# Low parts moved to GpSimd, a block's normed rows turned through DRAM, and a denser first weave

## The chip, the core and the metric

The kernel runs on one core of one Trainium2 chip. Its engines are TensorE (PE in the profile), VectorE (DVE), ScalarE (ACT), GpSimd (POOL) and SyncE (SP), whose queue issues nearly all transfers. The metric is the device time of one execution in microseconds, as the median of several runs.

## What is computed

Two layers, each a hedgehog linear attention and a squared-ReLU MLP, both with a layer norm ahead and a residual around them. S = 2048 rows, D = 576, H = 32 heads of 18, F = 4608.

```python
x = A_x
for layer in range(2):
    n = layernorm(x)
    q, k, v = n @ wqkv                      # split in 32 heads
    phi(u) = concat(softmax(u @ w_phi), softmax(-(u @ w_phi)))
    kv = phi(k)^T v;  z = sum of phi(k) over the rows
    x = x + (phi(q) kv / (phi(q) z + 1e-6)) @ wo
    n = layernorm(x)
    h = relu(n @ w1 + b1)
    x = x + (h * h) @ w2 + b2
```

All is fp32. The kernel holds each operand of a product as a high and a low part (the low is the value less its high part) and makes three products of them.

## The kernel before

The 2048 rows are four blocks of 512 (four tiles of 128 rows each), and a layer takes them in an order of its own: 3, 2, 0, 1 in layer 0 and 1, 0, 3, 2 in layer 1. The MLP of one block runs over 36 feature tiles f of 128 columns. For each tile `first` loads w1's columns and w2's rows and splits them: ACT makes the high parts (L1167 for w1, L1168 and L1169 for w2), DVE the low part of w1 (L1171, 128x640) and of 448 columns of w2 (L1174), POOL the low part of w2's other 128 columns (L1175). `hidden` is the first half of a tile on PE (14 matmuls, L1190); ACT then takes relu (L1197), square (L1198) and the square once more in full (L1199), and DVE the low part of that (L1200); the second half is `by_rows` (12 matmuls, L1217) and `features` (3, L1208), one tile behind the first half as the program is written.

The MLP of a layer's first block is woven with the attention of its second and third: `weave` lets the attention's generators go on by so many units of cost after each of the MLP's 36 yields. In this first weave (names m_3 in layer 0, m_1 in layer 1) run in turn the features of the second block (a_2 in layer 0, a_0 in layer 1), the query products and features of the third (a_0, then a_3), and then, for the second block, the output products (`o_product`: eight of 14 matmuls on PE, L999), the residual sum (`o_add` on DVE, L1004), and the layer norm `g_norm`: statistics on DVE (L459, L462), the root on POOL (L463, L464), the normed rows on DVE (L490, and L495 for the last 64 columns, written twice), x + b2 on POOL (L1051), transposes on PE (L512, L526) and the splits of their results on ACT and DVE (L520, L521, L533, L534). The turned rows, named a_2nh and a_2nl, are the operands of the next block's MLP (m_2), which is the second weave. The output products of a tile go through a few places in PSUM, which DVE's sums empty.

The features of the attention take another way to be turned: DVE transposes in blocks of 32x32 (L897), and stores put the blocks in their order in DRAM (L900), from which they are loaded.

A scheduler sets the order of instructions on each engine at build time. Each engine takes its own list strictly in that order; what is not ready holds what stands behind it.

## Time and profile before

| what | us |
|---|---|
| median of three runs | 2440.04 (2438.57 to 2442.45) |
| the profiled execution | 2441.59, span 2439.9 |
| PE busy | 2410.0 |
| DVE busy | 1560.5 |
| ACT busy | 1289.7 |
| POOL busy | 940.6 |
| first weave, layer 0 | 234 to 502 |
| second weave, layer 0 | 502 to 813 |
| first weave, layer 1 | 1441 to 1710 |
| second weave, layer 1 | 1710 to 2022 |

In a timeline a row holds the start, the time, the engine, the line, the operation, what is written from what, the shapes, and in brackets how long the engine stood idle before it and what it waited for last. Matmuls are pipelined, so that the time of one is longer than the distance to the next; distances between starts tell what PE spends. In a table by window the columns are the window, its length, busy time of the engines, the granted clock of PE (1.00 is full), the share of the transfer engines and GB/s.

### The profile page before, as it was taken

To read this page: it belongs to the slowest core of one execution; us is meant where nothing else is said; L and a number is where in the kernel's file an instruction comes from. 1 tells how busy PE (TensorE), PEld (TensorE's weight loads), DVE (VectorE), ACT (ScalarE), POOL (GpSimd) and SP (SyncE) were. 2 spreads that over 40 slices of the span, in tenths; PEclk is the share of its full clock that TensorE was granted. 3 is DMA by queue.
4 is the path that set the end of the run, shared out by engine and by line. 5 is a ranking of instruction groups with operands and counts; after the bars stand their busy time and mean duration, and the time that the engine had idled before them with its cause. 6 is when DMAs were issued, how large, how long until landed. Compare 5 with 4: busy or idle time off the path is not lost. (4 is left out here: it accounts for less than half of the span.)

```text
span 2439.9 us, 41475 instructions
## 1 busy us (share of the span) xinstructions
PE 2410.0 (99%) x14806; PEld 2137.9 (88%) x14806; DVE 1560.5 (64%) x2537; ACT 1289.7 (53%) x2543; POOL 940.6 (39%) x1121
## 2 busy tenths in 40 slices
PE   9999999999999999999999999999999999999999
PEld 8999888888888888888999988888887888888898
DVE  8779847664867655545766787486557675555443
ACT  4344555444456666664443444554455466676643
POOL 4555303212335565542433442032222455565321
PEclk9999999999999999999999999999999999999999
DMA  9124573666654533338753156537667444333364
GB/s 338 64 84 165 163 194 97 151 202 220 155 173 136 157 99 115 109 104 302 257 188 139 59 173 143 168 96 186 191 233 158 141 142 145 118 103 116 110 199 130
DMA packets 370646, 379.40 MB, mean 155 GB/s; under 512 B 142886, under 2 KB 270790, under 8 KB 367878
## 3 DMA queue, kind: packets, MB, share of 16 engines
q1 hardware_dynamic: 369180, 375.37, 51.2%
q8 instruction: 116, 1.90, 0.3%
q10 hardware_dynamic: 1258, 1.37, 0.2%
q14 instruction: 92, 0.75, 0.1%
HBM read 297.22 MB, written 79.41 MB: 154 GB/s over the span
## 5 line engine op out<-in xcount | busy, mean ns | idle before, releaser
L1507 POOL TENSOR_TENSOR m_ps<-m_pr,m_ps 128x128 fp32r<-128x128 f32 x144 | 98.6, 685 | 337.8 <-ACT m_ps L1505 310.7
L1506 DVE TENSOR_TENSOR m_ps<-m_pr,m_ps 128x448 fp32r<-128x448 f32 x144 | 99.8, 693 | 175.9 <-ACT m_ps L1504 175.8
L1549 PE MATMUL m_pacc<-m_ps,m_phb 128*128 128x448 f32 x864 | 185.6, 363 | 0.0
L1549 PEld LDWEIGHTS m_pacc<-m_ps,m_phb 128*128 128x128 f32 x864 | 161.9, 188 | 15.0
L1549 PE MATMUL m_pacacc<-m_ps,m_phc 128*128 128x448 f32 x648 | 147.1, 365 | 0.0
L1504 ACT ACTIVATE m_ps<-m_pr 128x448 fp32r<-128x448 f32 x144 | 82.8, 575 | 115.7 <-issue 64.9
L1549 PEld LDWEIGHTS m_pacacc<-m_ps,m_phc 128*128 128x128 f32 x648 | 119.2, 188 | 7.7
L1190 PE MATMUL m_0ph<-a_0nh,m_0h 128*128 128x512 f32 (+1 forms) x380 | 96.7, 382 | 1.6 <-ACT m_0hr L1197 1.4
L1190 PE MATMUL m_1ph<-t1onh,m_1h 128*128 128x512 f32 (+1 forms) x380 | 96.2, 381 | 2.0 <-ACT m_1hr L1197 1.8
L1217 PE MATMUL m_2acc<-m_2s,m_2hb 128*128 128x448 f32 x432 | 95.2, 367 | 2.9 <-ACT m_2s L1168 2.6
L1190 PE MATMUL m_3ph<-t0onh,m_3h 128*128 128x512 f32 (+1 forms) x380 | 96.1, 381 | 1.8 <-ACT m_3hr L1197 1.6
L1217 PE MATMUL m_0acc<-m_0s,m_0hb 128*128 128x448 f32 x432 | 95.0, 367 | 2.9 <-ACT m_0s L1168 2.6
L1190 PE MATMUL m_2ph<-a_2nh,m_2h 128*128 128x512 f32 (+1 forms) x380 | 96.6, 382 | 0.8 <-ACT m_2hr L1197 0.6
L1217 PE MATMUL m_3acc<-m_3s,m_3hb 128*128 128x448 f32 x432 | 94.2, 364 | 2.0 <-ACT m_3hb L1198 1.4
L1217 PE MATMUL m_1acc<-m_1s,m_1hb 128*128 128x448 f32 x432 | 94.2, 364 | 2.0 <-ACT m_1hb L1198 1.4
L1217 PEld LDWEIGHTS m_2acc<-m_2s,m_2hb 128*128 128x128 f32 x432 | 81.8, 190 | 11.7 <-ACT m_2s L1168 3.0
L1217 PEld LDWEIGHTS m_0acc<-m_0s,m_0hb 128*128 128x128 f32 x432 | 81.5, 190 | 11.7 <-ACT m_0s L1168 3.0
L1217 PEld LDWEIGHTS m_3acc<-m_3s,m_3hb 128*128 128x128 f32 x432 | 80.4, 188 | 10.6 <-ACT m_3hb L1198 2.1
L1217 PEld LDWEIGHTS m_1acc<-m_1s,m_1hb 128*128 128x128 f32 x432 | 80.4, 188 | 10.5 <-ACT m_1hb L1198 2.1
L1175 POOL TENSOR_TENSOR m_3s<-m_3r,m_3s 128x128 fp32r<-128x128 f32 x36 | 22.9, 637 | 161.9 <-ACT m_3s L1169 153.3
L1175 POOL TENSOR_TENSOR m_1s<-m_1r,m_1s 128x128 fp32r<-128x128 f32 x36 | 22.8, 635 | 162.0 <-ACT m_1s L1169 151.8
L1190 PEld LDWEIGHTS m_1ph<-t1onh,m_1h 128*128 128x128 f32 x380 | 68.8, 188 | 17.4 <-ACT m_1hr L1197 3.0
(2464 smaller groups left out, 7237.0 us busy)
## 6 DMA issues: line engine op xcount, KB each, us to landing
m_pr<-in_B_w SPq DMA_DIRECT2D x144, 288.0 KB
m_pr<-in_B_w SPq DMA_DIRECT2D x72, 256.0 KB
hd<-m_pu SPq DMA_DIRECT2D x72, 256.0 KB
m_pg<-hd SPq DMA_DIRECT2D x72, 256.0 KB
m_3r<-in_B_w SPq DMA_DIRECT2D x36, 288.0 KB
m_2r<-in_B_w SPq DMA_DIRECT2D x36, 288.0 KB
m_1r<-in_B_w SPq DMA_DIRECT2D x36, 288.0 KB
m_0r<-in_B_w SPq DMA_DIRECT2D x36, 288.0 KB
```

Of the source, the lines that this page charges most:

```text
L1175: nc.gpsimd.tensor_sub(s2[:, FC + P : FC + 2 * P], r2[:, R:], s2[:, FC : FC + P].bitcast(F32))
L1190: dense["hidden"] = nc.tensor.matmul(ph[:, cols], a, m, start=(k == 0), stop=(k == len(ops) - 1))
L1217: nc.tensor.matmul(acc[t][:, :R], a[:, rows], m, start=(f == 0 and k == 0), stop=(f == NF - 1 and k == 2))
L1504: nc.scalar.activation(s2[:, RO : RO + R], r2[:, :R], AF.Copy)
L1506: nc.vector.tensor_sub(s2[:, RO + R : RO + 2 * R], r2[:, :R], s2[:, RO : RO + R].bitcast(F32))
L1507: nc.gpsimd.tensor_sub(s2[:, FC + P : FC + 2 * P], r2[:, R:], s2[:, FC : FC + P].bitcast(F32))
L1549: nc.tensor.matmul(accs[b][t][:, :R], a[:, rows], m, start=(g == 0 and k == 0), stop=(g == NF - 1 and k == 2))
```

## The change

It has three parts. The low part of w2's 448 columns moves from DVE to POOL (for the first two tiles of a layer's first block it stays on DVE), in `low`. The norm of the first woven block is no longer `g_norm` but the new `g_norm_far`: one DVE operation norms all 576 columns, one more transposes them in blocks of 32x32, 16 stores per block put the pieces in order in DRAM, one load of 1 MB brings back the first 512 columns turned, `load_twice` the last 64 in two copies, and ACT and DVE split what came back. And the weave's rate goes from 3.7 to 4.2 units per yield.

```diff
--- before.py
+++ after.py
@@ -584,6 +584,56 @@
                 apart(NT - 1)
                 yield 1.6
 
+    def blocks_out(home, flat, t):
+        for i in range(NQ):
+            at = t * P + 32 * i
+            nc.sync.dma_start(home[:, at : at + 32].rearrange("(j f) r -> f j r", f=32),
+                              flat[32 * i : 32 * i + 32].rearrange("f (j r) -> f j r", r=32))
+
+    def g_norm_far(x_of, dst, name, then=None):
+        home = dram.tile([D, TB], F32, name=f"{name}xt")
+        xns, raw = {}, {}
+
+        def rows(t):
+            x = x_of(t)
+            mv, rstd = moments(x, t, name)
+            xns[t] = sb.tile([P, D], F32, tag="qk", name=f"{name}n{t}", bufs=5)
+            nc.vector.tensor_scalar(xns[t], x, mv[:, 0:1], rstd, op0=ALU.subtract, op1=ALU.mult)
+            if then:
+                then(t, x)
+
+        def turn(t):
+            nc.vector.transpose(xns[t], xns[t])
+
+        def store(t):
+            blocks_out(home, xns.pop(t), t)
+
+        def land():
+            dst.update(xt_tiles(name))
+            nc.sync.dma_start(dst["l"].bitcast(F32), home[: KC * P].rearrange("(c p) n -> p c n", p=P))
+            raw["t"] = sb.tile([P, TB], F32, tag="ft", name=f"{name}t", bufs=4)
+            load_twice(raw["t"], home, 0, TB)
+
+        def split(c):
+            if c < KC:
+                hi, src, p = dst["h"][:, c], dst["l"][:, c].bitcast(F32), slice(0, P)
+                lo = dst["l"][:, c]
+            else:
+                hi, src, p = dst["h"][:, c], raw["t"], slice(DT, P)
+                lo = dst["h"][DT:, c]
+            nc.scalar.activation(hi, src, AF.Copy)
+            dense["normed"] = nc.vector.tensor_sub(lo, src[p], hi[p].bitcast(F32))
+
+        yield from pipeline(NT, (rows, turn, lambda t: t < NT - 1 and store(t)), (3.0, 0.9, 0.2))
+        yield 3.0
+        store(NT - 1)
+        yield 3.0
+        land()
+        yield 4.0
+        for c in range(NC):
+            split(c)
+            yield 0.8
+
     def spill(b, x):
         nc.sync.dma_start(xth[b], x["h"].rearrange("p c n -> p (c n)").bitcast(F32))
         nc.sync.dma_start(xtl[b], x["l"].rearrange("p c n -> p (c n)").bitcast(F32))
@@ -895,10 +945,7 @@
         def turn(t):
             flat = ph[t].rearrange("p s d -> p (s d)")
             nc.vector.transpose(flat, flat)
-            for i in range(NQ):
-                at = t * P + 32 * i
-                nc.sync.dma_start(home[:, at : at + 32].rearrange("(j f) r -> f j r", f=32),
-                                  flat[32 * i : 32 * i + 32].rearrange("f (j r) -> f j r", r=32))
+            blocks_out(home, ph[t].rearrange("p s d -> p (s d)"), t)
 
         yield from held(pipeline(NT, (start, lambda t: soft_exp(ph[t]), add, factors, lambda t: phi_scale(ph[t], rs[t]),
                                       turn), (2.6, 0.4, 3.0, 2.8, 1.2, 1.6)), ("last", "squared"))
@@ -1171,7 +1218,7 @@
                 dense["lowered"] = (nc.gpsimd if early else nc.vector).tensor_sub(l1, r1, h1.bitcast(F32))
 
             def low():
-                nc.vector.tensor_sub(s2[:, RO + R : RO + 2 * R], r2[:, :R], s2[:, RO : RO + R].bitcast(F32))
+                (nc.vector if early else nc.gpsimd).tensor_sub(s2[:, RO + R : RO + 2 * R], r2[:, :R], s2[:, RO : RO + R].bitcast(F32))
                 nc.gpsimd.tensor_sub(s2[:, FC + P : FC + 2 * P], r2[:, R:], s2[:, FC : FC + P].bitcast(F32))
 
             if early:
@@ -1839,7 +1886,7 @@
         def back_first():
             m, later = f"a{layer}_{order[2]}", []
             mid = (g_queries(layer, order[2], None, later, m), g_features(layer, later, early, m))
-            yield from g_attend(layer, order[1], None, raws, nxt, f"a{layer}_{order[1]}", dense, None, mid)
+            yield from g_attend(layer, order[1], None, raws, nxt, f"a{layer}_{order[1]}", dense, g_norm_far, mid)
 
         def back_second():
             yield from g_attend(layer, order[2], None, None, operands, f"a{layer}_{order[2]}", None,
@@ -1923,7 +1970,7 @@
                 if last:
                     keep.update(x=xk, es=es, v=wpair("v", f"w{m}"))
 
-        weave(g_mlp(layer, order[0], ready, [], f"m{layer}_{order[0]}", dense.pop("rest")), chained(back_first()), 3.7, "rows")
+        weave(g_mlp(layer, order[0], ready, [], f"m{layer}_{order[0]}", dense.pop("rest")), chained(back_first()), 4.2, "rows")
         back = chained(back_second())
 
         def then():
```

The lines shift by 47 from `first` on: w1's low is L1218 then, w2's L1221 and L1222, the first half L1237, the second L1264 and L1255, relu, square and full square L1244 to L1246, the output products L1046 and their sums L1051. The new lines are L601 (normed rows), L606 (transpose on DVE), L590 (stores), L613 (load) and L624 and L625 (splits).

Three places show how the order of instructions changes. The first is DVE in the first weave of layer 0, where the output products of the last tiles are summed and normed (a_2x rows with the residual, a_2ns and a_2nm their statistics, a_2nn the normed rows, m_3h and m_3s the split w1 and w2 of a feature tile, whose number follows). Before:

```order
L1004 TENSOR_TENSOR a_2x_5698<-a_2po_5716,a_2x_5698 128x288 [waits PE_49]
L459 BN_STATS a_2ns_5732<-a_2x_5698 128x6 [waits DVE_49]
L462 BN_AGGR a_2nm_5733<-a_2ns_5732 128x2 [waits DVE_49]
L490 TENSOR_SCALAR a_2nn_5740<-a_2x_5698,a_2nm_5733,a_2nd_5734 128x512 [waits DVE_49,Pool_49]
L1174 TENSOR_TENSOR m_3s_30_5436<-m_3r_30_5430,m_3s_30_5436 128x448 [waits DMAHW4_49,Activation_49]
L495 TENSOR_SCALAR a_2ne<-a_2x_5698,a_2nm_5733,a_2nd_5734 128x128
L1171 TENSOR_TENSOR m_3h_31_5494<-m_3r_31_5488,m_3h_31_5494 128x640 [waits DMAHW6_49,DMAHW7_49,DMAHW5_49,Activation_49]
L1174 TENSOR_TENSOR m_3s_31_5495<-m_3r_31_5489,m_3s_31_5495 128x448 [waits DMAHW0_49,Activation_49]
```

The last of these rows is the low part of w2 for f=31, and behind it the weave runs on for three more feature tiles before the last two tiles of rows come. With the change:

```order
L1051 TENSOR_TENSOR a_2x_5700<-a_2po_5702,a_2x_5700 128x288 [waits PE_49]
L459 BN_STATS a_2ns_5734<-a_2x_5700 128x6 [waits DVE_49]
L1051 TENSOR_TENSOR a_2x_5700<-a_2po_5718,a_2x_5700 128x288 [waits PE_49]
L459 BN_STATS a_2ns_5734<-a_2x_5700 128x6 [waits DVE_49]
L462 BN_AGGR a_2nm_5735<-a_2ns_5734 128x2 [waits DVE_49]
L601 TENSOR_SCALAR a_2nn_5742<-a_2x_5700,a_2nm_5735,a_2nd_5736 128x576 [waits DVE_49,Pool_49]
L606 STREAM_TRANSPOSE a_2nn_5742<-a_2nn_5742 128x576 [waits DVE_49]
L1218 TENSOR_TENSOR m_3h_28_5351<-m_3r_28_5345,m_3h_28_5351 128x640 [waits DMAHW6_49,DMAHW7_49,DMAHW5_49,Activation_49]
L1247 TENSOR_TENSOR m_3hb_5477<-m_3hr_5476,m_3hb_5477 128x512 [waits Activation_49]
L1218 TENSOR_TENSOR m_3h_29_5453<-m_3r_29_5447,m_3h_29_5453 128x640 [waits DMAHW6_49,DMAHW7_49,DMAHW0_49,Activation_49]
```

The four tiles of rows now stand in one run, the fourth of them shown here, and w1's low for f=28 has moved behind the whole run. No w2 low stands among these rows.

The second place is PE, at the tiles 32 and 33 of the same block (m_3ph the first half's sums, m_3acc the second's). Before:

```order
L1190 MATMUL m_3ph_5564<-t0onh,m_3h_32_5556 128x512 [waits Activation_49]
L1190 MATMUL m_3ph_5564<-t0onh,m_3h_32_5556 128x512 x4
L1190 MATMUL m_3ph_5564<-t0onl,m_3h_32_5556 128x512 x4
L1190 MATMUL m_3ph_5564<-t0onh,m_3h_32_5556 128x512 [waits DVE_49]
L1190 MATMUL m_3ph_5564<-t0onh,m_3h_32_5556 128x512 x4
L1190 MATMUL m_3ph_5662<-t0onh,m_3h_33_5654 128x512 [waits Activation_49]
L1190 MATMUL m_3ph_5662<-t0onh,m_3h_33_5654 128x512 x4
L1190 MATMUL m_3ph_5662<-t0onl,m_3h_33_5654 128x512 x4
L1190 MATMUL m_3ph_5662<-t0onh,m_3h_33_5654 128x512 [waits DVE_49]
L1190 MATMUL m_3ph_5662<-t0onh,m_3h_33_5654 128x512 x4
L1217 MATMUL m_3acc_3539<-m_3s_32_5557,m_3hb_5678 128x448 [waits Activation_49]
```

The second half of f=32 has the first half of f=33 ahead of it. With the change:

```order
L1237 MATMUL m_3ph_5760<-t0onh,m_3h_32_5752 128x512 [waits Activation_49]
L1237 MATMUL m_3ph_5760<-t0onh,m_3h_32_5752 128x512 x4
L1237 MATMUL m_3ph_5760<-t0onl,m_3h_32_5752 128x512 x4
L1237 MATMUL m_3ph_5760<-t0onh,m_3h_32_5752 128x512 [waits DVE_49]
L1237 MATMUL m_3ph_5760<-t0onh,m_3h_32_5752 128x512 x4
L1264 MATMUL m_3acc_3539<-m_3s_32_5753,m_3hb_5831 128x448 [waits Activation_49]
L1264 MATMUL m_3acc_3539<-m_3s_32_5753,m_3hb_5831 128x448 [waits Pool_49]
L1264 MATMUL m_3acc_3540<-m_3s_32_5753,m_3hb_5831 128x448 x2
L1264 MATMUL m_3acc_3541<-m_3s_32_5753,m_3hb_5831 128x448 x2
L1264 MATMUL m_3acc_3542<-m_3s_32_5753,m_3hb_5831 128x448 x2
L1264 MATMUL m_3acc_3539<-m_3s_32_5753,m_3hb_5831 128x448 [waits DVE_49]
```

The second half of f=32 now follows its own first half. So it is for f=28, 33 and 34, and the second half of f=31 stands behind the last three matmuls of f=30. Going back to the run of output products, f=27's second half stands inside it, and f=28's first half right behind it. Further up, the query products of the third block have moved two feature tiles earlier; the direct successions of that region were f=13's two halves and f=14 and 15's first halves, and are now the first halves of f=12 and f=13.

The third place is SP's queue at the end of the same weave, with the fourth tile's stores (a_2nxt is the place in DRAM, m_3r the loaded weights):

```order
L1208 DMA m_3r_33_5802<-in_B_w 128x576 [waits DMAHW0_49,Pool_49]
L590 DMA a_2nxt<-a_2nn_5742 32x18x32 [waits DMAHW1_49]
L590 DMA a_2nxt<-a_2nn_5742 32x18x32 [waits DMAHW2_49]
L590 DMA a_2nxt<-a_2nn_5742 32x18x32 [waits DMAHW3_49]
L590 DMA a_2nxt<-a_2nn_5742 32x18x32 [waits DMAHW4_49]
L1206 DMA m_3r_34_5861<-in_B_w 128x4x128 [waits DMAHW5_49,DVE_49]
L244 DMA m_3r_34_5861<-in_B_w 64x128 [waits DMAHW6_49]
L244 DMA m_3r_34_5861<-in_B_w 64x128 [waits DMAHW7_49]
L613 DMA a_2nl<-a_2nxt 128x4x512 [waits DMAHW2_49,DMAHW3_49,DMAHW1_49,DMAHW4_49,DMAHW0_49,PE_49]
L244 DMA a_2nt<-a_2nxt 64x512 x2
L1208 DMA m_3r_34_5862<-in_B_w 128x576 [waits Pool_49]
```

None of the stores and loads of a_2nxt stood there before; the weight loads around them did. The load of the turned rows now stands between the w1 and the w2 loads of f=34. On ACT, the first two splits (L624) have come to stand behind w1's high part of f=34 and ahead of the relu of f=34.

## The prediction

> **What bounds the kernel now.** I read the page's totals first, then a table by stage, then the waits of TensorE (PE) with its timeline.
>
> ```profile
> span 2439.9 us, 41475 instructions
> ...
> PE 2410.0 (99%) x14806; PEld 2137.9 (88%) x14806; DVE 1560.5 (64%) x2537; ACT 1289.7 (53%) x2543; POOL 940.6 (39%) x1121
> ```
>
> PE is busy for all but 30 us, so a change gains only what it takes from PE's instructions or from those 30 us, and loses what it adds to them.
>
> ```profile
> core 0: us, PE busy (x) PEld busy (x) DVE busy (x) ACT busy (x) POOL busy (x), PEclk, DMA share, GB/s
> 234.00:502.00 268.00, 264.27 (x1314) 229.99 (x1313) 185.04 (x274) 139.12 (x255) 71.20 (x74) 1.00 0.60 157
> 1441.00:1710.00 269.00, 265.07 (x1319) 230.50 (x1318) 186.72 (x276) 139.78 (x257) 71.43 (x74) 1.00 0.59 158
> ```
>
> These stretches are the first weaves of the two layers, where the change lies. Each has under 4 us of idle PE, so there is little to win and everything that opens between matmuls is new time. The idle pieces of layer 0 are these:
>
> ```profile
> 320.31 2.68 PE L1217 MATMUL m_3acc<-m_3s,m_3hb 128*128 128x448 f32 x12 [1.44 <-ACT m_3hb L1198]
> ...
> 327.64 1.45 PE L1190 MATMUL m_3ph<-t0onh,m_3h 128*128 128x512 f32 x5 [0.78 <-ACT m_3hr L1197]
> ...
> 455.05 0.40 PE L999 MATMUL a_2po<-a_2o0h,a_2oh 126*128 126x288 f32 x1 [0.18 <-DVE a_2x L1004]
> ...
> 457.99 1.27 PE L1217 MATMUL m_3acc<-m_3s,m_3hb 128*128 128x448 f32 x5 [0.56 <-DVE m_3s L1174]
> ...
> 471.60 1.45 PE L1190 MATMUL m_3ph<-t0onh,m_3h 128*128 128x512 f32 x5 [0.78 <-ACT m_3hr L1197]
> ...
> 503.95 0.86 PE L1190 MATMUL m_2ph<-a_2nh,m_2h 128*128 128x256 f32 x5 [0.19 <-DVE a_2nl L521]
> ```
>
> They give the two prices that carry my sum. Where the second half of feature tile f stands directly behind its own first half (f=13, at 320.31), PE waits 1.44 us for relu and square on ACT. Where the first half of f+1 stands directly behind the first half of f, it waits 0.78 us for the relu.
>
> **The work that PE does meanwhile.**
>
> ```profile
> 446.79 0.29 PE L999 MATMUL a_2po<-a_2o0h,a_2oh 126*128 126x288 f32 x1
> ...
> 454.26 0.60 PE L512 MATMUL a_2np<-ident,a_2nn 128*128 128x128 f32 x4
> ...
> 459.11 1.29 PE L1190 MATMUL m_3ph<-t0onh,m_3h 128*128 128x512 f32 x5
> ...
> 462.28 0.77 PE L1217 MATMUL m_3acc<-m_3s,m_3hb 128*128 128x448 f32 x3
> ...
> 463.89 2.67 PE L1217 MATMUL m_3acc<-m_3s,m_3hb 128*128 128x448 f32 x12
> ...
> 467.07 0.29 PE L999 MATMUL a_2po<-a_2o0h,a_2oh 126*128 126x288 f32 x1
> ```
>
> Starts against starts: a first half takes 462.28 - 459.11 = 3.17 us, a second half 467.07 - 463.89 = 3.18, and four output products (446.79 to 454.26) 7.47, so one is 1.87. The last three matmuls of a second half are some 0.69 of it.
>
> **Part 1: transposes leave PE.**
>
> ```profile
> L512 PE MATMUL a_2np<-ident,a_2nn x16: 270/272/278, 454.3 to 501.5; 128*128 128x128 f32 x16
> ...
> L526 PE MATMUL a_2np<-ident,a_2ne x4: 272/273/273, 491.9 to 501.7; 128*128 128x128 f32 x4
> ```
>
> ```profile
> 491.07 0.60 PE L512 MATMUL a_2np<-ident,a_2nn 128*128 128x128 f32 x4
> 491.42 0.65 PE L1217 MATMUL m_3acc<-m_3s,m_3hb 128*128 128x448 f32 x2
> ```
>
> The matmuls overlap: four take 0.35 us from start to start, not 4 x 0.27. Twenty take 20 x 0.0875 = 1.75 us a layer. That is the whole direct gain of this part, 3.5 us in both layers.
>
> **Part 2: the DRAM trip.** Sixteen stores, one large load and two tail loads join SP's queue.
>
> ```profile
> 450.37 3.13 SPq L900 DMA_DIRECT2D a_0ft<-a_0Q3e  x4
> ```
>
> ```profile
> 1875.18 10.45 DMA a_2w<-a_2ft
> ```
>
> The same kind of store takes 0.78 us to issue, so 19 issues hold SP for up to 15 us, over some 45 us. Tile 3's stores stand behind the w2 load of f=33, which waits for GpSimd's low of f=31. By the walk of part 3 f=28's w1 low ends 24.7 us after the first output product; f=31's loads follow it, f=31's low on GpSimd comes at some 35, and so the last stores at about 41 and the load at 47 (an estimate). I take 8 to 10 us for the load, from the 10.45 us row (504 KB, the nearest): it is there at about 56. ACT's first split stands behind f=33's squares, by the same walk at about 64. So the trip costs nothing, with 8 us of cover; if the cover is gone, ACT's relu of f=34 is queued behind that split and PE waits one for one.
>
> **Part 3: the denser weave and the order it makes.** The output products of four tiles now come in one run, from f=27 instead of f=29, and nothing is left over to separate the last feature tiles. I walk the new order with the durations above; 0 is the first output product. The durations on DVE and POOL come from their timelines and from the groups of this stage.
>
> ```profile
> 449.96 0.42 DVE L1004 TENSOR_TENSOR a_2x<-a_2po,a_2x 128x288 f32<-128x288 f32 x1
> 450.42 0.46 DVE L459 BATCH_NORM_STATS2 a_2ns<-a_2x 128x6 f32<-128x288 f32 x1
> ...
> 451.76 0.21 DVE L462 BATCH_NORM_AGGREGATE a_2nm<-a_2ns 128x2 f32<-128x12 f32 x1
> 452.97 0.55 DVE L490 TENSOR_SCALAR a_2nn<-a_2x,a_2nm,a_2nd 128x512 f32<-128x512 f32 x1 [1.00 <-POOL a_2nd L464]
> ...
> 458.12 0.81 DVE L1171 TENSOR_TENSOR m_3h<-m_3r,m_3h 128x640 fp32r<-128x640 f32 x1
> ```
>
> ```profile
> L1174 DVE TENSOR_TENSOR m_3s<-m_3r,m_3s 128x448 fp32r<-128x448 f32 x36 | 26.9, 751 | 3.1 <-ACT m_3s L1168 3.0
> ...
> L897 DVE STREAM_TRANSPOSE a_0Q3e<-a_0Q3e 128x1152 f32<-128x1152 f32 x1 | 1.4, 1379 | 0.1
> ```
>
> ```profile
> L1175 POOL TENSOR_TENSOR m_3s<-m_3r,m_3s 128x128 fp32r<-128x128 f32 x36 | 22.9, 637 | 161.9 <-ACT m_3s L1169 153.3 <-DMA m_3r<-in_B_w 5.5 <-DVE m_3h L1171 3.1
> ...
> L1171 POOL TENSOR_TENSOR m_3h<-m_3r,m_3h 128x640 fp32r<-128x640 f32 x2 | 3.1, 1567 | 5.4 <-ACT m_3h L1167 5.4
> ```
>
> - The fifth product waits for a place that DVE must empty. Before, this cost 0.18 behind 0.35 us of transposes; without them 0.5.
> - f=27's second half, in the middle of the products, waits for GpSimd's 128x448 low, which stands behind tile 1's two small POOL steps. No row shows that operation; between POOL's 128x128 (0.64) and 128x640 (1.57) I take 1.2. The low ends about 1.3 us after PE wants it (bounds 0 and 2).
> - f=28's first half needs its w1 low from DVE, which now stands behind the norm and transpose of all four tiles. Eight products, f=27 and the waits so far end at 15.0 + 3.2 + 1.8 = 20.0; nine matmuls of f=28 run on to 22.0. DVE needs from 20.0: add 0.45, stats 0.46, aggregate 0.21, 1.0 for POOL's root, some 0.65 for 576 columns, 0.7 for the transpose (half the 128x1152 row), 0.81 for the low: 24.3, with semaphores 24.7. Wait 2.7 (2.3 to 3.1).
> - Then f=28's second half directly behind its first: 1.44. f=30 behind f=29: 0.78. f=31's second half has only three matmuls ahead of it: 1.44 - 0.69 = 0.75. f=32, 33 and 34 each follow directly: 3 x 1.44 = 4.32.
> - The handover to the next block: one relu wait at most, 0.8 (0 to 0.8).
>
> Together 0.5 + 1.3 + 2.7 + 1.44 + 0.78 + 0.75 + 4.32 + 0.8 = 12.6 us a layer. Against that, the pieces of 455.05, 457.99, 471.60 and 503.95 go (0.18 + 0.56 + 0.78 + 0.19 = 1.7), and so does the 1.44 at 320.31, since the query products now stand between f=13's halves; the 0.78 there stays, between f=12 and f=13. Those query products come two feature tiles earlier (2 x 6.35 us), with their loads far ahead in SP's queue: 0. ACT's splits are five of 512 columns instead of six, beside PE work as before: 0.
>
> **Part 4: w2's low on GpSimd.** 140 subtractions leave DVE (36 in a weave are 26.9 us, 0.75 each; f=0 and 1 of the first block stay). DVE is 64% busy, so its relief is worth nothing by itself. GpSimd does the wide and the narrow part one after the other, 1.2 + 0.64 = 1.8 us, and each tile's matmuls start, less the end of its low, nearly always 7 to 20 us later. Two had no such room: f=30 (at 457.99, counted above) and f=17 in the second weave:
>
> ```profile
> 659.47 0.49 PE L1217 MATMUL m_2acc<-m_2s,m_2hb 128*128 128x448 f32 x1 [2.57 <-ACT m_2s L1168]
> 660.26 3.83 PE L1217 MATMUL m_2acc<-m_2s,m_2hb 128*128 128x448 f32 x11 [0.30 <-DVE m_2s L1174]
> ```
>
> There 1.2 for 0.62, starting a little sooner, adds about 0.45 a layer (0 to 1.3).
>
> **The clock after a long gap.** The row above is also the one gap of the size that I forecast for f=28.
>
> ```profile
> 659.50:660.30 0.80, 0.50 (x2) 0.20 (x2) 0.71 (x2) 0.12 (x1) 0.61 (x1) 0.68 0.83 286
> 660.30:664.00 3.70, 3.70 (x12) 3.33 (x13) 0.62 (x1) 0.78 (x2) 0.92 (x2) 0.61 1.37 204
> 664.00:668.00 4.00, 4.00 (x21) 3.54 (x20) 1.45 (x2) 1.52 (x3) 0.43 (x1) 1.00 0.89 280
> ```
>
> The clock column falls to 0.61 behind it and is back at 1.00 from 664. Half speed over 3.4 us costs 1.7 us. If it comes behind f=28's wait in both layers, 3.4 us are added; I give that half a chance and leave it out of the sum. The Trainium skill, page "TensorE: Matmul & The Clock Gate", section "Part 1: The HAM clock gate", says that the clock is set by a free-running window of about 3.4 us and halves after an idle one; by a threshold of a whole idle window a wait of 2.7 us would never do it and the sum would stand. This trace disagrees: 2.57 us were enough here.
>
> **Sum.** 12.6 - 1.7 - 1.44 - 1.75 + 0.45 = 8.2 us a layer, 16.3 in both. The profiled execution took 2441.6 us (span 2439.9), 1.6 above the median of the runs, 2440.0. So 2441.6 + 16.3 = 2458 by it, 2456 by the median; I say 2457. What is late next: DVE's w1 lows of f=29 and 30 follow f=28's and SP's loads of f=31 and 32 wait for them, still ahead of PE by my count.
>
> **Rivals.**
> - The succession costs nothing, so it ends faster. Its mechanism: DVE and ACT are early enough that relu and square overlap PE's last matmuls. For: DVE loses 27 us of lows in this weave. Against: relu cannot start before the half's last matmul, and the one direct succession in the trace paid 1.44. It decides once the new waits stay under 4.4 us a layer (1.7 + 1.44 + 1.75 - 0.45). With none, 2440.0 - 8.9 = 2431; with 2.5 a layer left, 2436.
> - Only ACT's successions hold, and the DVE and POOL waits of the products (0.5 + 1.3 + 2.7) and the handover shrink to nothing: 12.6 - 5.3 = 7.3, so +2.9 a layer, 2446.
> - The trip lands late. Its price is one for one beyond 64 us; SP's queue, in which stores wait behind weight loads that wait for GpSimd, could be 12 us later than I count. Then ACT holds f=34's relu by 4 us a layer, and 2457 + 8 = 2465.
> - GpSimd becomes late for several feature tiles, because DVE and POOL slow each other:
>
> ```profile
> 458.28 1.95 POOL L1051 TENSOR_TENSOR a_2x<-a_2x,b2t 128x576 f32<-128x576 f32 x1 [1.15 <-DVE a_2ne L495]
> 458.85 1.85 DVE L1174 TENSOR_TENSOR m_3s<-m_3r,m_3s 128x448 fp32r<-128x448 f32 x1
> ```
>
> That 1.85 stands beside a 128x576 sum on POOL. With each low at 2 instead of 1.2 the tightest ones (f=17, 27, 28) pay 0.8 each: 2.4 a layer, 2462. The Trainium skill, page "SBUF — State Buffer", section "SBUF: two separate sides", calls the port pair of the two engines an exclusive lock, held for a whole instruction, which these two rows bear out.
>
> **From these to the numbers.** My forecast, with or without the halved clock (2457 to 2460): 0.57. Late trip: 0.12. Late GpSimd: 0.08. Successions alone: 0.10. Faster: 0.13. The range of 8 in 10 leaves out most of the faster case and the far end of the late ones: 2437 to 2466. Within 0.2% (4.9 us), which is about what a measurement can tell from no change, lie a half-faster case and the low edge of the successions: 0.10. Faster 0.13, slower 0.77.
>
> **What would show it.** Right: PE idle of 12 to 13 us in each first weave instead of 3.7, with 1.4 us pieces released by the square before f=32, 33 and 34, and one of some 2.7 us released by DVE in f=28; no matmul into a_2np; ACT's first split of a_2nh without a DMA wait. Wrong: pieces under 0.5 us before those tiles, or a DMA as releaser of ACT, or stalls in the second weave on POOL.

## The result and the profile after

The changed kernel took 2485.13 us (median of four runs, 2482.92 to 2485.49), beside 2440.26 us (2438.57 to 2442.45) for the kernel before on the same chip. The ratio is 1.0181, with a 95% interval from 1.0164 to 1.0199. The forecast was 2457 with a range of 2437 to 2466: the direction came out, the size did not. 17 us were expected, 45 came. I begin with the page of the changed kernel and the table by stage:

```profile
span 2483.1 us, 41200 instructions
...
PE 2423.2 (98%) x14766; PEld 2141.4 (86%) x14766; DVE 1491.7 (60%) x2395; ACT 1290.4 (52%) x2541; POOL 1092.1 (44%) x1261
```

```profile
core 0: us, PE busy (x) PEld busy (x) DVE busy (x) ACT busy (x) POOL busy (x), PEclk, DMA share, GB/s
234.00:502.00 268.00, 254.92 (x1239) 219.28 (x1239) 161.15 (x227) 128.94 (x233) 105.07 (x103) 0.99 0.59 150
1441.00:1710.00 269.00, 259.26 (x1328) 225.48 (x1327) 175.22 (x273) 127.54 (x239) 111.68 (x113) 0.98 0.58 149
...
456.00:462.50 6.50, 5.06 (x14) 4.09 (x13) 2.68 (x3) 3.87 (x7) 2.59 (x3) 0.50 0.88 212
507.00:510.20 3.20, 2.91 (x8) 2.61 (x9) 3.17 (x4) 2.07 (x5) 2.36 (x3) 0.53 0.31 81
...
1685.00:1695.00 10.00, 7.76 (x19) 6.16 (x20) 3.42 (x4) 3.87 (x7) 4.48 (x5) 0.50 0.66 158
```

PE's idle time has grown from 30 us to 60 (span less busy), and PE is also *busy* 13 us longer, with 40 matmuls fewer. The second part is seen in the last three rows: behind two of the gaps of layer 0, and behind the like of the first in layer 1, the granted clock is about 0.5. (The second row covers other work than the row with the same times before, since everything there is some 24 us later.) The waits of PE in the first weave of layer 0, and the costliest of them in the timeline (in square brackets: the idle time ahead of a piece and what ended it):

```profile
engine line waited for: us in total, times, longest us
PE m_3acc L1264 <- ACT m_3hb L1245: 5.1, 4, 1.4
PE m_3ph L1237 <- DVE m_3h L1218: 3.6, 1, 3.6
PE m_3ph L1237 <- ACT m_3hr L1244: 2.7, 3, 1.1
PE m_3acc L1264 <- ACT m_3s L1215: 2.3, 1, 2.3
PE m_3acc L1264 <- POOL m_3s L1221: 1.4, 2, 1.0
```

```profile
247.70 1.43 PE L1237 MATMUL m_3ph<-t0onh,m_3h 128*128 128x512 f32 x5 [1.09 <-ACT m_3hr L1244]
...
440.80 2.08 PE L1264 MATMUL m_3acc<-m_3s,m_3hb 128*128 128x448 f32 x9 [1.03 <-POOL m_3s L1221]
...
454.91 1.59 PE L1237 MATMUL m_3ph<-t0onh,m_3h 128*128 128x512 f32 x5 [3.56 <-DVE m_3h L1218]
457.93 4.85 PE L1264 MATMUL m_3acc<-m_3s,m_3hb 128*128 128x448 f32 x12 [1.44 <-ACT m_3hb L1245]
...
489.23 2.68 PE L1264 MATMUL m_3acc<-m_3s,m_3hb 128*128 128x448 f32 x12 [1.44 <-ACT m_3hb L1245]
...
506.06 0.88 PE L1264 MATMUL m_3acc<-m_3s,m_3hb 128*128 128x448 f32 x3 [2.28 <-ACT m_3s L1215]
507.29 2.98 PE L1264 MATMUL m_3acc<-m_3s,m_3hb 128*128 128x448 f32 x7 [0.35 <-POOL m_3s L1221]
```

The kernel before had 3.7 us of such waits in this weave; here it is 15.9, and layer 1 has nearly the same pieces. The second half at 457.93 takes 4.85 us instead of 2.7: that is the halved clock.

Setting the starts of like matmuls of the two traces against each other gives where the 43.2 us of span arise: some 16.7 in the first weave of layer 0 with its handover (a first half that started at 536.06 starts at 553.03; 0.3 of that stands ahead of the weave), 2.5 in its second weave, 5.2 in a stretch ahead of layer 1's first weave (1402 to 1441 us), and 16.9 and 1.9 in the two weaves of layer 1. In layer 0's second weave PE's waits are 6.1 us for 4.2. The 5.2 us are no part of the change's mechanism; they are taken up under the padded kernel below.

### The profile page after: what moved, and what is told of

The parts are those of the page before. It is cut to its first block, busy times and chain, and to the rows that moved or that the text cites. A ratio compares the mean times of both kernels' runs of the same rounds, so it can differ in the third digit from the quotient of the medians.

```text
span 2483.1 us, 41200 instructions
## 1 busy us (share of the span) xinstructions
PE 2423.2 (98%) x14766; PEld 2141.4 (86%) x14766; DVE 1491.7 (60%) x2395; ACT 1290.4 (52%) x2541; POOL 1092.1 (44%) x1261
## 3 DMA queue, kind: packets, MB, share of 16 engines
q10 hardware_dynamic: 1258, 1.37, 0.2%
## 4 chain that ended last, share of the span: by engine, by line
PE 85%; DVE 4%; POOL 3%; DMA 3%; ACT 3%; issue 2%; SPq 1%; ACTq 0%; POOLq 0%; DVEq 0%
PE m_ppx L1564 9%; PE m_pacc L1596 7%; PE m_pacacc L1596 5%; PE m_ppy L1564 4%; PE m_3ph L1237 4%; PE m_1ph L1237 4%; PE m_2ph L1237 3%; PE m_0ph L1237 3%; PE m_3acc L1264 3%; PE m_1acc L1264 3%; PE m_2acc L1264 3%; PE m_0acc L1264 2%; PE m_ppz L1564 2%; PE m_pacc L1586 2%; PE m_pacacc L1586 2%
## 5 line engine op out<-in xcount | busy, mean ns | idle before, releaser
L1264 PE MATMUL m_3acc<-m_3s,m_3hb 128*128 128x448 f32 x432 | 98.1, 374 | 8.7 <-ACT m_3hb L1245 5.1
L1264 PE MATMUL m_1acc<-m_1s,m_1hb 128*128 128x448 f32 x432 | 98.0, 374 | 8.7 <-ACT m_1hb L1245 5.1
L1221 POOL TENSOR_TENSOR m_1s<-m_1r,m_1s 128x448 fp32r<-128x448 f32 x34 | 44.1, 1296 | 139.6 <-ACT m_1s L1215 129.0
L1221 POOL TENSOR_TENSOR m_3s<-m_3r,m_3s 128x448 fp32r<-128x448 f32 x34 | 43.9, 1290 | 138.1 <-ACT m_3s L1215 127.9
L1237 PE MATMUL m_1ph<-t1onh,m_1h 128*128 128x512 f32 (+1 forms) x380 | 98.0, 387 | 6.5 <-DVE m_1h L1218 3.5
L1237 PE MATMUL m_3ph<-t0onh,m_3h 128*128 128x512 f32 (+1 forms) x380 | 97.0, 383 | 6.4 <-DVE m_3h L1218 3.6
L1264 PEld LDWEIGHTS m_3acc<-m_3s,m_3hb 128*128 128x128 f32 x432 | 82.8, 194 | 19.7 <-ACT m_3hb L1245 6.9
L1264 PEld LDWEIGHTS m_1acc<-m_1s,m_1hb 128*128 128x128 f32 x432 | 82.7, 193 | 19.7 <-ACT m_1hb L1245 7.1
L1237 PE MATMUL m_0ph<-a_0nh,m_0h 128*128 128x512 f32 (+1 forms) x380 | 97.0, 383 | 1.8 <-ACT m_0hr L1244 1.2
L1237 PE MATMUL m_2ph<-a_2nh,m_2h 128*128 128x512 f32 (+1 forms) x380 | 96.8, 383 | 1.6 <-ACT m_2hr L1244 1.2
L1264 PE MATMUL m_2acc<-m_2s,m_2hb 128*128 128x448 f32 x432 | 95.0, 367 | 3.4 <-ACT m_2s L1215 2.6
L1264 PE MATMUL m_0acc<-m_0s,m_0hb 128*128 128x448 f32 x432 | 95.0, 367 | 3.4 <-ACT m_0s L1215 2.6
L1221 POOL TENSOR_TENSOR m_0s<-m_0r,m_0s 128x448 fp32r<-128x448 f32 x36 | 43.2, 1199 | 113.6 <-ACT m_0s L1215 111.8
L1221 POOL TENSOR_TENSOR m_2s<-m_2r,m_2s 128x448 fp32r<-128x448 f32 x36 | 43.1, 1197 | 112.1 <-ACT m_2s L1215 110.3
L1264 PEld LDWEIGHTS m_2acc<-m_2s,m_2hb 128*128 128x128 f32 x432 | 82.0, 190 | 11.7 <-ACT m_2s L1215 3.0
```

What stands on the lines that cost most here:

```text
L1221: (nc.vector if early else nc.gpsimd).tensor_sub(s2[:, RO + R : RO + 2 * R], r2[:, :R], s2[:, RO : RO + R].bitcast(F32))
L1237: dense["hidden"] = nc.tensor.matmul(ph[:, cols], a, m, start=(k == 0), stop=(k == len(ops) - 1))
L1264: nc.tensor.matmul(acc[t][:, :R], a[:, rows], m, start=(f == 0 and k == 0), stop=(f == NF - 1 and k == 2))
```

## The experiments

The change has three parts, and I first took them apart. "Rate" is the density of the first weave (3.7 before, 4.2 after), "far" the turn by DVE with the trip through DRAM, "low" w2's wide low part on GpSimd. All ratios are to runs of the kernel before on the same chip, with 95% intervals.

| kernel | median us | ratio | interval |
|---|---|---|---|
| before + rate | 2444.56 | 1.0011 | 1.0001 to 1.0020 |
| before + low | 2454.23 | 1.0048 | 1.0033 to 1.0063 |
| before + far | 2490.78 | 1.0201 | 1.0183 to 1.0219 |
| before + far + rate | 2473.13 | 1.0126 | 1.0111 to 1.0141 |
| all three (the change) | 2485.13 | 1.0181 | 1.0164 to 1.0199 |

**The rate alone**, on the kernel before:

```diff
-        weave(g_mlp(...), chained(back_first()), 3.7, "rows")
+        weave(g_mlp(...), chained(back_first()), 4.2, "rows")
```

> The kernel before with the rate 4.2 alone: transposes stay on PE, w2's lows stay on DVE. Theory (the loss comes from the denser rate and the far norm together): PE's list has two direct successions (f=28's halves at 1.44, f=29 to 30 at 0.78) where before had 0.78 + 1.44 + 0.78, and f=28's w1 low stands behind two tiles' norms instead of four, a wait of 1 us or less: 2440 to 2446. Rival (the rate alone does it): about 2475 to 2485.

It cost 2.5 us and PE's waits in the first weave stay as before (one square, two relus). So the denser weave does not make the successions by itself.

**The low alone**, on the kernel before:

```diff
-                nc.vector.tensor_sub(s2[:, RO + R : RO + 2 * R], r2[:, :R], ...)
+                (nc.vector if early else nc.gpsimd).tensor_sub(s2[:, RO + R : RO + 2 * R], r2[:, :R], ...)
```

> The kernel before with w2's wide low on GpSimd alone; PE's list is unchanged. Theory: only the lows without room pay, f=17 of the second weave (0.78 on GpSimd instead of 0.30) and one or two of the first: 2440 to 2443. Rival (GpSimd is the new bound or slows DVE everywhere): 2455 or more.

It cost 12.2 us, where the prediction's Part 4 had 0.9, and came out close to the rival's 2455. Its timeline shows why, at two places (POOL, ACT and PE at the start of the weave; POOL, DVE and PE at the handover to the next block):

```profile
244.29 1.63 POOL L1221 TENSOR_TENSOR m_3s<-m_3r,m_3s 128x448 fp32r<-128x448 f32 x1 [4.31 <-ACT m_3s L1215]
246.30 1.69 POOL L703 TENSOR_TENSOR a_2Q0e<-a_2Q0m,t0q2qs 128x576 f32<-128x576 f32 x1
248.02 1.16 ACT L707 ACTIVATE a_2Q0e<-a_2Q0e 128x1152 f32<-128x1152 f32 x1 [3.61 <-POOL a_2Q0e L703]
249.82 1.43 PE L1237 MATMUL m_3ph<-t0onh,m_3h 128*128 128x512 f32 x5 [1.09 <-ACT m_3hr L1244]
...
503.85 1.15 POOL L1221 TENSOR_TENSOR m_2s<-m_2r,m_2s 128x448 fp32r<-128x448 f32 x1
503.92 1.36 DVE L490 TENSOR_SCALAR a_2nn<-a_2x,a_2nm,a_2nd 128x512 f32<-128x512 f32 x1 [0.43 <-POOL a_2nd L464]
509.25 0.86 PE L1237 MATMUL m_2ph<-a_2nh,m_2h 128*128 128x256 f32 x5 [0.89 <-DVE a_2nl L521]
```

At 244.29 the low stands on POOL ahead of a sum for the features; ACT waits for that sum 3.61 us (1.94 before) with its exponential, PE's relu is queued behind the exponential, and PE waits 1.09. At 503.92 it is not a queue: the norm on DVE runs beside POOL's low and takes 1.36 us instead of 0.81, and PE waits 0.89 instead of 0.19. PE's matmuls that use the low itself are hardly held. The low's own consumer, which is all that I had looked at, is not where the price lies.

To place it, the low was moved in the first blocks only, and in the second blocks only:

```diff
-                nc.vector.tensor_sub(s2[:, RO + R : RO + 2 * R], ...)
+                (nc.gpsimd if rest and not early else nc.vector).tensor_sub(s2[:, RO + R : RO + 2 * R], ...)   # first
+                (nc.vector if rest else nc.gpsimd).tensor_sub(s2[:, RO + R : RO + 2 * R], ...)                # second
```

> The kernel before with w2's wide low on GpSimd in the first block of each layer only. Theory (GpSimd's queue and the lock between the two engines: the low stands ahead of other GpSimd work and slows DVE at a few places): the pieces seen with all lows moved, 1.09 at the start, 0.85 for 0.56 at the output products, 0.9 at the handover, so 1.7 to 2.3 a layer: 2445 to 2447. Rival (the two blocks act on each other, or the loss has another place): no more than 2443, or 2450 and more.

> The kernel before with w2's wide low on GpSimd in the second block of each layer only. Theory: the rest of the 12 us, 2.5 to 5 a layer from f=17's low (0.78 for 0.30) and the norm and query pieces on GpSimd behind lows: 2448 to 2451, so that the two halves add up to 12. Rival: no more than 2444.

First blocks: 2446.22 us, 1.0018 [1.0008, 1.0027]. Second blocks: 2449.54, 1.0033 [1.0020, 1.0046]. The two add up, 4.4 + 7.7 = 12.1. The wait at the weave's start goes with the first, the one at the handover with the second (one row of each trace):

```profile
247.37 1.43 PE L1237 MATMUL m_3ph<-t0onh,m_3h 128*128 128x512 f32 x5 [1.14 <-ACT m_3hr L1244]
```

```profile
504.98 0.86 PE L1237 MATMUL m_2ph<-a_2nh,m_2h 128*128 128x256 f32 x5 [0.89 <-DVE a_2nl L521]
```

**The far norm alone**, at the old rate, on the kernel before:

```diff
-            yield from g_attend(..., dense, None, mid)
+            yield from g_attend(..., dense, g_norm_far, mid)
```

> The kernel before with the turn through DRAM alone, rate 3.7: no transposes of that block on PE and no direct succession at the end of the weave, but the last stores and the load stand behind the last feature tile in SP's queue. Theory: the trip is then bare, some 13 to 15 us of idle PE between the last second half and the next block, and one half-clock stretch, in each layer: 2464 to 2475. Rival (the trip is hidden here too, and the loss came from the rate): 2435 to 2438.

```profile
512.81 0.39 SPq L613 DMA_DIRECT2D a_2nl<-a_2nxt  x1
...
519.45 2.19 ACT L624 ACTIVATE a_2nh<-a_2nl 128x512 fp32r<-128x512 f32 x4 [3.72 <-DMA a_2nl<-a_2nxt]
...
520.13 2.14 PE L1237 MATMUL m_2ph<-a_2nh,m_2h 128*128 128x256 f32 x4 [13.22 <-ACT a_2nh L624]
```

Here the trip is bare: the load is issued at 512.81, ACT's split waits for it, and PE stands still for 13.22 us in layer 0 and 12.8 in layer 1. The whole change's trace has the load issued at 485.18 and ACT's first split at 498.37 without a wait for it (the row below). So the prediction's rival of the late trip holds at the old rate and not at the new one.

```profile
498.37 1.14 ACT L624 ACTIVATE a_2nh<-a_2nl 128x512 fp32r<-128x512 f32 x2
```

It took 2490.78 us, more than the 2464 to 2475 expected. Three things come on top of the trip in this trace: the wait of 3.56 us for a w1 low of DVE stands here too (at 479.24, and 3.55 in layer 1), the clock is at 0.50 for 17.1 us around the end of each standstill (510.1 to 527.2 in layer 0), and PE stops for 3.57 us in layer 1's keys, as told under the padded kernel.

**Far and rate together**, the low left on DVE (the changed kernel, with one line back as it was):

```diff
-                (nc.vector if early else nc.gpsimd).tensor_sub(s2[:, RO + R : RO + 2 * R], ...)
+                nc.vector.tensor_sub(s2[:, RO + R : RO + 2 * R], ...)
```

> The change without the move to GpSimd: far norm and rate 4.2; PE's list is that of the changed kernel. Theory: the waits of the successions stay, f=27's wait for POOL goes and f=28's w1 low, behind as many DVE operations, stays late: 2476 to 2485. Rival (GpSimd's lows are a large part of the loss): below 2465.

2473.13 us, a little less than expected: the rate gives 17.6 us of the far norm's loss back, and what the low adds to this kernel is 12.0 by the medians, as much as alone. That is in part chance. Of the 13.6 us between the spans of the two traces 4.5 lie at PE's stop in layer 1's keys, which lasted 1.33 us here and 3.48 in the changed kernel; nearly all of the other 9 lie in the weaves. PE's waits in the first weave:

```profile
PE m_3acc L1264 <- ACT m_3hb L1245: 5.1, 4, 1.4
PE m_3ph L1237 <- DVE m_3h L1218: 3.6, 1, 3.6
PE m_3acc L1264 <- ACT m_3s L1215: 2.3, 1, 2.3
```

The four successions (5.1 us), f=28's wait for its w1 low (3.6) and f=34's (2.3) are all here. f=28's wait belongs to the far norm, which has it at the old rate too. The successions at the end and f=34's wait belong to far and rate together: the rate has to empty the weave's end, so that the trip is covered, and so nothing is left to stand between the halves of the last feature tiles.

**The clock behind f=28's wait.** In the changed kernel the first nine matmuls of f=28's first half in the first blocks are run twice, so that PE has work in the gap; the second pass starts the sum anew.

```diff
+            if f == 28 and rest:
+                for k, (a, m) in enumerate(ops[: NC + KC]):
+                    nc.tensor.matmul(ph[:, cols], a, m, start=(k == 0), stop=(k == NC + KC - 1))
```

> The changed kernel, but in the first woven block PE runs the first nine matmuls of f=28's first half twice (the second time from a fresh start, so the result stays). They fall into the 3.56 us in which PE waits for f=28's w1 low from DVE. Theory (a long gap halves the clock for about 6.8 us, cost 2.5 to 3.4 us a layer): the gap falls to about 1.5 us, f=28 ends at the same time, the clock stays at 1.00 behind it: 2478 to 2481. Rival 1 (the clock falls with or without the gap): 2484 to 2486. Rival 2 (the extra matmuls are not covered): 2 x 2.05 more, 2489.

2477.41 us, 1.0140 [1.0121, 1.0159]: eighteen matmuls more, and 7.7 us less than the changed kernel (34.9 above the kernel before on its own chip, for 44.9).

```profile
454.93 1.45 PE L1240 MATMUL m_3ph<-t0onh,m_3h 128*128 128x512 f32 x5 [1.52 <-DVE m_3h L1218]
```

```profile
456.00:462.50 6.50, 5.06 (x24) 4.14 (x23) 2.69 (x3) 4.65 (x9) 3.20 (x4) 1.00 0.92 219
```

The dependent matmul starts at the same time as in the changed kernel (454.93 and 454.91), so the wait itself is not shortened; but the clock stays at 1.00 and 24 matmuls run in the window that had 14. The halved clock is a cost of its own, shown by taking it away: by like matmuls the kernel gains 2.4 us behind f=28 in layer 0 and 3.6 in layer 1. (Other parts of the difference lie elsewhere, see the padded kernel.)

**Why f=28 waits 3.56 us and not 2.7.** The low that it waits for took 1.42 us on DVE instead of the 0.81 of my walk. DVE and POOL in the changed kernel:

```profile
452.11 0.58 DVE L601 TENSOR_SCALAR a_2nn<-a_2x,a_2nm,a_2nd 128x576 f32<-128x576 f32 x1 [1.00 <-POOL a_2nd L464]
...
453.43 1.42 DVE L1218 TENSOR_TENSOR m_3h<-m_3r,m_3h 128x640 fp32r<-128x640 f32 x1
...
452.77 1.40 POOL L1098 TENSOR_TENSOR a_2x<-a_2x,b2t 128x576 f32<-128x576 f32 x1 [0.70 <-DVE a_2nn L601]
454.13 1.72 POOL L1221 TENSOR_TENSOR m_3s<-m_3r,m_3s 128x448 fp32r<-128x448 f32 x1
```

POOL's sum runs until 454.17 and DVE's low ends 0.68 us later, at 454.85; POOL's next low, begun meanwhile, takes 1.72. The Trainium skill, page "SBUF — State Buffer", section "SBUF: two separate sides", calls the shared port pair an exclusive lock held for a whole instruction; these rows agree. To try it, POOL's sum was left out, so that b2 is missing in those rows of the output:

```diff
         def keep(t, x):
-            nc.gpsimd.tensor_add(x, x, b2t)
+            if norm is not g_norm_far:
+                nc.gpsimd.tensor_add(x, x, b2t)
```

> The changed kernel without the sum x + b2 on GpSimd for the first woven block of each layer (b2 is missing in those rows' output). PE's list is unchanged. Theory (DVE and GpSimd hold each other up): f=28's w1 low on DVE, 1.42 us beside the fourth sum, goes back to about 0.82, PE's wait of 3.56 falls to about 2.9, f=27's wait for POOL stays near 1.0: 2479 to 2484, the lower end if the halved stretch behind gets shorter too. Rival (1.42 has another cause): the wait stays at 3.5, 2484 to 2486.

```profile
452.09 1.37 DVE L601 TENSOR_SCALAR a_2nn<-a_2x,a_2nm,a_2nd 128x576 f32<-128x576 f32 x1 [1.00 <-POOL a_2nd L464]
...
454.20 0.78 DVE L1219 TENSOR_TENSOR m_3h<-m_3r,m_3h 128x640 fp32r<-128x640 f32 x1
...
452.02 1.13 POOL L1222 TENSOR_TENSOR m_3s<-m_3r,m_3s 128x448 fp32r<-128x448 f32 x1
...
455.03 2.50 PE L1238 MATMUL m_3ph<-t0onh,m_3h 128*128 128x512 f32 x5 [3.71 <-DVE m_3h L1219]
```

2483.87 us, 1.0167 [1.0147, 1.0188], not to be told from the change. The low took 0.78 as expected, but POOL's own low moved forward into the norm on DVE, which took 1.37 instead of 0.58. The hold-up went from one instruction of the chain to another, and the wait stayed (3.71). My expectation had only the one collision in view.

**Spreading the run of tiles.** On far and rate with the low on DVE, the cost of a tile's rows in the pipeline was doubled, with two rates:

```diff
-        yield from pipeline(NT, (rows, turn, lambda t: t < NT - 1 and store(t)), (3.0, 0.9, 0.2))
+        yield from pipeline(NT, (rows, turn, lambda t: t < NT - 1 and store(t)), (6.0, 0.9, 0.2))
...
-        weave(..., chained(back_first()), 4.2, "rows")
+        weave(..., chained(back_first()), 4.4, "rows")   # and 4.2
```

> Far norm with w2's lows on DVE, rate 4.4, and a tile of normed rows charged with 6.0 instead of 3.0 units, so that the rest of the norm is spread over the last feature tiles. PE's list then has four direct successions (f=11 1.44, f=13 0.78, f=28 0.78, f=35 1.44) instead of f=28, 30, 31, 32, 33, 34 at 8.7 together, and the load stands ahead of the last feature tile. Theory (the successions and the late w1 low cost what far norm and rate cost, the trip nothing when it is early): 2438 to 2448. Rival (the trip or the stores themselves slow the weave): 2460 or more.

> As the run before, but rate 4.2: successions f=13 0.78, f=28 1.44, f=30 0.78 only, w1's low of f=28 behind all four tiles on DVE, and the load and splits behind the last feature tile on SP and ACT. Theory: the wait for f=28 stays (3.5 us and the halved clock), the successions of f=31 to 34 go, the trip is bare for 3 to 8 us in each layer: 2455 to 2468. Rival (the successions never mattered): 2473 or more.

At rate 4.4 it took 2469.65 us, 1.0108 [1.0089, 1.0127], some 4 us better than far and rate (27.2 above the kernel before, for 31.1), where 2438 to 2448 was expected; at 4.2 2481.52, 1.0156 [1.0135, 1.0177], above the 2455 to 2468 expected. By like matmuls the first won more, some 9 us in the weaves: PE's stop ahead of layer 1 cost 5.3 us in its trace and 0.8 in that of far and rate. In the first the successions at the end are gone, but f=28's first half still waits behind the tiles on DVE; in the second the trip is late again, with PE waiting at the start of the next block (6.77 us in layer 1 too):

```profile
450.08 1.43 PE L1237 MATMUL m_3ph<-t0onh,m_3h 128*128 128x512 f32 x5 [3.57 <-DVE m_3h L1218]
...
506.13 1.00 PE L1255 MATMUL m_3acc<-m_3hb,m_3s 128*128 128x512 f32 x2 [1.81 <-ACT m_3hb L1245]
```

```profile
516.39 1.44 PE L1237 MATMUL m_2ph<-a_2nh,m_2h 128*128 128x256 f32 x5 [6.78 <-ACT m_2h L1214]
```

The second came out at its rival's number, but not by the rival's cause: its trace has no direct succession behind f=30 left to pay, and beside the late trip the clock is at 0.50 for 6.8 us in each layer there, and PE's stop costs 4.6 us. So what spacing wins at one end it pays at the other. No kernel of this study beats the one before.

**The 5.2 us ahead of layer 1.** In layer 1's keys PE stops, with nothing that it waits for in the timeline ("issue"), and runs at half clock behind it. The place in the program differs from kernel to kernel, but it always comes behind PE's 9535th recorded matmul: in the changed kernel after 13 of 64 small products (kvp); with nine matmuls more in layer 0, after 4 of 64. To move it, 20 matmuls of 128x128 were put at f=28, in layer 0 alone, as many as the transposes that the change took away there:

```diff
+            if f == 28 and rest and layer == 0:
+                for k in range(20):
+                    nc.tensor.matmul(ph[:, :P], h1[:, 0], xh[:, 0, :P], start=(k == 0), stop=(k == 19))
```

> The changed kernel with 20 small matmuls more on PE in layer 0 only (128x128 into f=28's sums ahead of its first half, which starts afresh behind them), as many as the transposes that the change took away there. They lie in the 3.56 us wait. In every run without those transposes PE stands for 0.9 to 3.6 us ahead of its 9535th matmul in the keys of layer 1, with no wait on another engine. Theory (the place is fixed by the count of instructions, a border of PE's code): with the count restored it goes back between the query products, 0.6 or less, and the halved clock behind it goes too, 4.6 us; with 1.7 us of the wait filled, layer 0's first weave gains 1 to 3: 2477 to 2480. Rival (it belongs to the keys, or to the transfers of that moment): the pause of about 3 us stays at the same kvp products: 2482 to 2484.

2476.29 us, 1.0141 [1.0124, 1.0158], 9 us less than the change (34.5 above the kernel before on its own chip). The stop in the changed kernel with the two microseconds behind it, with nine matmuls more, with twenty more, and in far and rate:

```profile
1409.95 1.05 PE L753 MATMUL kvp<-k_lastK3e,vs 128*32 128x36 f32 x51 [3.48 <-issue]
```

```profile
1410.00:1412.00 2.00, 2.00 (x55) 1.92 (x56) 0.31 (x1) 0.97 (x2) 0.00 (x0) 0.50 0.74 244
```

```profile
1407.31 0.74 PE L753 MATMUL kvp<-k_lastK3e,vs 128*32 128x36 f32 x60 [0.91 <-issue]
```

```profile
1405.60 0.53 PE L656 MATMUL t1q0qp<-t1q0h,n_0l 128*128 128x288 f32 x2 [1.16 <-issue]
```

```profile
1403.76 0.66 PE L753 MATMUL kvp<-k_lastK3e,vs 128*32 128x36 f32 x51 [1.33 <-issue]
```

With twenty more, the stop lies between query products, where the kernel before has its own (0.60 us, at 1386.41). There it costs little: by like matmuls the padded kernel loses 0.7 us over the stretch that cost 5.2. But the place alone does not decide the cost. In far and rate the stop lies at the same small product as in the changed kernel, and cost 0.8. What goes with the cost is the length: the five traces with a stop of 3.0 to 3.6 us all have the clock at 0.50 behind it and lose 3.7 to 5.5 us there, those with one of 0.9 to 1.3 keep the clock at 1.00 and lose 0.3 to 0.8 (all by like matmuls, against the kernel before). The four kernels with the transposes on PE and another part changed (rate, low, and the low in one block) have no stop at this count at all.

What PE waited for can be read from the transfers. The page counts a queue of its own for instructions, q8, with 115 packets of 16 KB; its columns are packets, MB and share. In the changed kernel one of them moves from 1407.38 to 1408.58, during the stop, and in far and rate from 1401.27 to 1402.22 (the rows of 1407.3 to 1408.6 and of 1401.2 to 1402.3):

```profile
q8 instruction: 1, 0.02, 5.7%
```

```profile
q8 instruction: 1, 0.02, 5.4%
```

In all thirteen traces it is the 74th packet of that queue. In the nine with a stop PE goes on 1.3 to 1.8 us after the packet's end; in the four without one the same matmul starts 1.8 to 2.9 us after it. So PE seems to wait for instructions that come late. That is argued from these times: no run moved the packet alone, and why it is later in some kernels stays open.

The gain of the nine and of the twenty is thus made mainly of two things, the clock behind f=28 and this stop. By like matmuls the nine gain 2.4 + 3.6 us behind f=28 in the two layers and 4.9 at the stop, and 1.5 because the clock stays at 1.00 behind f=34 in layer 0; some 3 us are lost again in layer 0's second weave. The twenty gain 2.4 behind f=28 in layer 0, 4.6 at the stop, and 1.2 in layer 1, where the clock is low for 6.8 us behind f=28 for 10.2.

## Why the prediction was wrong in size

- **Direction, and the waits of Part 3 in kind: right.** The price was carried by new waits in the first weaves, under the names given: the square before f=28, 32 and 33 at 1.44 us each, f=30 at 0.78, f=31 at 0.76 for 0.75. The fifth product waited 0.29 for 0.5, f=27's second half 1.03 for 1.3, the handover 0.54 for 0.8. The transposes left PE, no gain is seen from DVE's relief, and the trip was hidden. The walked terms sum to 13.9 us a layer, for 12.6 forecast.
- **Two of these terms were too small.** f=28's wait was 3.56 for 2.7 (outside its bounds, 2.3 to 3.1), because DVE's low came behind a sum on POOL and took 1.42 us for 0.81. A row of the prediction, with 1.85 us beside such a sum, had shown this, and I kept it for a rival. f=34's was 2.63 for 1.44: ACT had a split and a high part ahead of PE's need there, and the walk had counted the splits at 0.
- **The clock was left out of the sum.** I had a row for it, gave it half a chance and one stretch of 3.4 us. It came in both layers, behind f=28's gap for 6.8 us in layer 0 and 10.2 in layer 1, and behind f=34's for 3.4 in each. By the busy time in those windows that is some 2.7 + 1.7 us in layer 0 and 3.9 + 1.7 in layer 1, 10 in all (an estimate).
- **Part 4 failed.** w2's low on GpSimd was 0.45 us a layer and measured 12 us in all (9 in the weaves of the changed kernel, by like matmuls). The step that failed is "each tile's matmuls start, less the end of its low, nearly always 7 to 20 us later": that is the low's own consumer. Its price lay with what stands behind it on POOL (the sum at 246.30, and by ACT's queue the relu) and with what runs beside it on DVE. Of the 12 us the rows account for about 2 a layer at the two places above; f=17 (0.78 us of wait for 0.30 before) adds 0.5 a layer, and a wait of 1.19 for a relu at 794 in layer 0's second weave stands for one of 0.60 before. Of that trace's 13.0 us, 2.4 lie ahead of the first weave, where nothing was moved. The rest I did not follow, and its cause stays open. The duration itself was right (1.2 us estimated, 1.29 mean in the first layer's weaves). The rival that came nearest, GpSimd late for its own tiles, put the price in the wrong place as well.
- **Not foreseen:** 1.09 us near the weave's start (1.17 in layer 1), 0.46 at the query products of layer 0, and the 5.2 us at PE's stop in layer 1. And each gap makes the matmuls behind it a little slower: a second half takes 3.22 us from start to start behind a wait (481.22 to 484.44) and 3.11 without (470.89 to 474.00), which for nine gaps more (15 for 6) is some 1.0 us a layer, an estimate.
- **The rivals.** Successions for nothing and the faster case: refuted, since every direct succession paid. The late trip: refuted for the change, shown for the far norm at the old rate (13.2 us).

In layer 0 the first weave's waits grew by 12.2 us and the handover's by 0.3, the transposes give back 1.75, the clock takes 4.4 and the restarts 1.0: 16.2 of 16.7 measured there. In layer 1 it is 11.3 of waits, 5.6 of clock and the same others, 16.5 of 16.9. With 2.5 and 1.9 in the second weaves and 5.2 at PE's stop these are the 43.2 us.

## What to carry to other kernels

Where one engine is 99% busy, price a moved instruction by all three of its neighbours: who uses its result, what is queued behind it on its new engine, and what runs beside it on an engine that it was seen to hold up (here DVE and POOL). Of a gap on the matmul engine, put in the clock behind it as a term of the sum as soon as a row of the trace shows it for a gap of like size, and look whether a second gap follows before the clock has come back. A part of a change that only hides another's latency (here the denser weave) is not priced alone: alone it cost 2.5 us, with the far norm it gave 17.6 back and made the successions that cost more than the transposes had.

## What the hardware showed that I had not expected

- A gap of 3.56 us, followed by one of 1.44, kept the granted clock at 0.50 for 6.8 us in layer 0 and for 10.2 in layer 1; gaps of 2.28 and 0.35 us lowered it for 3.4 in both layers, and not at all in layer 0 of the filled kernel; single gaps of 1.44, and 1.52 followed by 1.44 in the filled kernel, never did. The Trainium skill, page "TensorE: Matmul & The Clock Gate", section "Part 1: The HAM clock gate", has a free-running window of about 3.4 us; the lengths of the slow stretches, one to three times that, agree with it, its threshold of a whole idle window does not.
- In nine of thirteen traces, one profiled execution each, PE stops behind its 9535th recorded matmul, for 0.6 to 3.6 us, with nothing to wait for in the timeline, and goes on 1.3 to 1.8 us after the end of the 74th packet of the instruction queue. A stop of 3 us and more, with the clock halved behind it, cost 3.7 to 5.5 us; shorter ones 0.8 at most. So a change in layer 0 went with 5 us in layer 1, and a comparison of two kernels here has to take the stop out first.
